# Denominators of two batches inverted once per head, and an order planned with other landing times

## The chip, the cores and the metric

The kernel runs on one core of a Trainium2 chip. Its engines are TensorE (PE, matrix products, with weight loads shown as PEld), VectorE (DVE), ScalarE (ACT), GpSimd (POOL, which here issues the loads) and SyncE (SP, which issues stores and DMA transposes). The metric is the device time of one execution in microseconds, as the median of several runs.

## The reference

Eight batches of eight heads; sequence S = 576, head dimension 64, 32 landmarks (means over 18 neighbouring positions). The attention is approximated through the landmarks, and its output goes through a layer of two products with a silu between them.

```python
m = 32
q_lm = q.reshape(B, H, m, S // m, D).mean(axis=3)
k_lm = k.reshape(B, H, m, S // m, D).mean(axis=3)
A  = sm(q, k_lm)          # softmax of scale * q k_lm^T, over the landmarks
Bm = sm(q_lm, k_lm)
C  = sm(q_lm, k)
Z  = Bm^T / (norms of Bm)
for _ in range(6):
    Z = 2 * Z - Z @ Bm @ Z
attn = A @ Z @ C @ v      # (8, 8, 576, 64)
x = attn.transpose(0, 2, 1, 3).reshape(4608, 512)
h = x @ w_in              # 512 x 2048
out = (h * sigmoid(h)) @ w_out   # 2048 x 512
```

The change concerns the softmax of A: the exponentials exp(scale * q k_lm^T) have to be divided by their sum over the 32 landmarks, for each query position of each head.

## The kernel before

Work goes batch by batch. The eight heads of a batch are two groups (g = 0, 1) of four; four heads times 32 landmarks fill the 128 partitions, so all tiles of the landmark side are "128 x positions". The 576 positions are handled as two halves (c = 0, 1) of HS = 288 columns.

For each batch, `attn(b)` lays down these steps, by the names that they have in the code and with the lines of the profile:

- loads of q, k and v by POOL (`ld...`, `ldv...`, L447 to L460; w_in and w_out L467 to L477);
- the transposed q and k, `qT`: for batches 0 to 2 by PE (L568) and a copy, from batch 3 on by DMA transposes on SP (`xt`, L592), which also wait for the second-last load of the batch's own v;
- landmark sums (`lms` on PE for batches 0 and 1, a tree of additions `red`, L628, on DVE for the others), the landmarks transposed (`ltr`, `lmT`), their product `sb` and its exponential `pb` (L688, L693);
- the iteration for Z: products `ns` on PE and the step `nsd` on DVE (L754), six times in turn;
- for A: products `A`, four exponentials `Ax` on ACT into `et` (L784), four products `S` with a mask of ones, `bones`, so that every one of a head's 32 partitions gets the sum over its landmarks, four logarithms `Ln` on ACT (L794, 288 columns each), two exponentials of minus that, `Rs` (L798, 576 columns each), which gives the reciprocals, and two products on DVE, `etn` (L803, 576 columns);
- for C: products `C`, exponentials `Cx` with their sums (L829), the transposed result `ct` (PE for batches 0 and 1, L844; DMA on SP after that, L856), and the product with v, `cv`;
- the small matrices joined (`wc` L889, `zbd` L894, `zt`), and the product `m` of the result with w_in, copied out by ACT (L404) or DVE (L406).

`layer1(b)` then multiplies `etn` with `m` (`h`, 16 tiles of 512 and two that gather the last 64 columns) and applies the silu on ACT into `gm` and `gx` (L956, L979). `layer2_batch(b)` multiplies by w_out: the first 256 positions of batch 0 plainly, the rest in pairs by seven products in place of eight with sums on DVE (L1044), evacuated by copies and additions (`ost`, L404, L406, L1079) and stored from SP (L1021).

Exponentials and logarithms are in one ACT table and the silu in another, so ACT goes through a group `x{b}` of one batch's exponentials as a whole before it changes the table (`ACT_TABLE_LOAD`, 1.28 us).

The order in which each engine gets its instructions is written by a planner in the kernel, `Plan.run`. It knows a duration for each operation and a lag before its result can be used; whenever an engine is free it picks the ready operation with the lowest priority value. A PE operation is ready only `margin` after its inputs (MARGIN = 0.4 us, nothing for those marked crit). The dict `ORDER` shifts the priority of 52 named operations; `o.done` of a load holds how long after its turn in the queue it lands, `XLAG` the same for DMA transposes. Engines then run their instructions strictly in the planned order, each waiting for its inputs by semaphores. Up to 45 us the planner fills free PE time with a product of zeros, tile `zer`.

`mm` (L394) is the helper of all products and `copy` (L404, L406) of all copies, so that tiles tell more than lines there.

Of the kernel before, what the change touches and what calls it, by code (L numbers as in the profile page):

```python
# [7 lines left out]
FP = mybir.dt.float32  # L8
# [8 lines left out]


ORDER = {
    "f0.0": (200.69, 0), "A.0": (-135.46, 12.93), "Ln11.0": (-57.289, 0), "etn1.0": (-31.554, 0),  # L20
    "ctm00.0": (-1364.2, 0), "wc.0": (-5319.5, 0), "mc11.0": (-629.91, 0), "tr10.1": (-42.668, 0),
    "trc15.1": (-1007.6, 0), "tr19.1": (-457.92, 0), "tr114.1": (-85.703, 0),
    "tr00.1": (-4845.1, 0), "tr09.1": (-1.1208, 0), "tr014.1": (-139.96, 0),
    "lms116.1": (413.98, 0), "lms000.1": (-607.71, 0), "lms006.1": (-83.37, 0),
    "lms010.1": (328.48, 0), "nsd00.1": (-627.38, 0), "ns10.1": (2306.7, 0),
    "nsd10.1": (-1204.8, 0), "A.1": (-266.77, 0), "Ax10.1": (-230.29, 0), "Rs1.1": (-127.11, 0),
    "Cx00.1": (-281, 0), "Cx01.1": (-181.38, 0), "Cx11.1": (-2693.4, 0), "tr014.2": (-314.54, 0),
    "bbd.2": (-120.57, 0), "nsd40.2": (175.02, 0), "h15.1": (234.98, 0), "lrd1.3": (-791.6, 0),
    "A.3": (-480.16, 0), "S00.3": (52.867, 0), "Ln01.3": (24.258, 0), "Ax11.3": (-2.2697, 0),
    "h3.2": (185.78, 0), "hx0.2": (41.862, 0), "h11.2": (452.76, 0), "hx8.2": (-6.3754, 0),  # L30
    "p5@5200.0": (-179, 0), "c12@5220.0": (-251.23, 0), "A.4": (-78.982, 0),
    "etn1.4": (1667.8, 0), "Cx11.4": (29.753, 0), "cv0.4": (-3300.5, 0),
    "p6@5340.0": (-4.9303, 0), "p7@5340.0": (-4146.8, 0), "Ax10.6": (162.02, 0),
    "ss00@5500.0": (-5226.2, 0), "p7@5700.0": (633.04, 0), "p4@5720.0": (524.17, 0),
}


# [29 lines left out]
class Plan:  # L67
# [16 lines left out]
    def run(self):  # L84
# [59 lines left out]
        while n < total:  # L144
# [7 lines left out]
            while moved:  # L152
                moved = False
                for e in ("PE", "ACT", "DVE", "POOL", "SP"):
# [101 lines left out]
                    lag = self.LAG[e] if o.lag is None else o.lag  # L256
                    if o.dma:
                        dmaq[0] = max(dmaq[0], end + 0.1) + o.dma
                        o.done = dmaq[0] + ((2.2 if t < 4.2 else 3.3 if t < 45 else 4.0)
                                              if e == "POOL" else lag)  # L260
                    else:
                        o.done = end + lag
# [39 lines left out]
def act_us(n):  # L302
    return 0.06 + 0.00083 * n
# [6 lines left out]
def mm_us(n, count=1):  # L310
    return count * max(n / 2400 + 0.0025, 0.028)
# [3 lines left out]
def kernel(  # L315
# [24 lines left out]
    SW = 128 + L  # L340
    NPE = 2
    NTR = 3
    SBF = 2
    MERGE = False
    WM = False
    NCT = 2
# [11 lines left out]
    def bank(o, i=0):  # L358
        return banks[o.slot[i]]
# [33 lines left out]
    def mm(out_ap, lhsT, rhs, start=True, stop=True):  # L393
        nc.tensor.matmul(out=out_ap, lhsT=lhsT, rhs=rhs, start=start, stop=stop,  # L394
                         skip_group_check=True)

    def bc(ap, n, axis):
        shape = list(ap.shape)
        shape.insert(axis, n)
        return ap.unsqueeze(axis).to_broadcast(shape)  # L400
# [128 lines left out]
    def folds(e):  # L529
        for r in (0, 64):  # L530
            for c in (0, 64):
                nc.vector.tensor_copy(out=fold[r:r + 64, c:c + 64], in_=idb[r:r + 64, r:r + 64])
    cfold = A("fold", [("DVE", 0.6)], folds, [cid], 90.0)


# [6 lines left out]
    def attn(b):  # L542
# [41 lines left out]
        else:  # L584
# [3 lines left out]
            for t in (1, 0):  # L588
                for g in range(NG):
                    qt_ops[t, g] = [A(  # L590
                        f"xt{t}{g}.{b}", [("SP", 1.38)],
                        lambda e, t=t, g=g: nc.sync.dma_start_transpose(  # L592
                            out=qT[:, t, g], in_=qk[:, t, g].rearrange("p j d -> p (j d)")),
                        [qk_ops[b, t, g]] + use + gate, p0 + 5, lag=XLAG)]
                    qt_ops[t, g][0].after = gate
                    me["qk_read"] += qt_ops[t, g]
                    me["xts"] += qt_ops[t, g]
# [170 lines left out]
        def am(e):  # L768
            for g in range(NG):
                for h in range(4):  # L770
# [5 lines left out]
                    lmT_all + ([] if cr else [(pb_op, -0.2)]) + qt_ops[0, 0] + qt_ops[0, 1] + ready, p0 + 20,  # L776
                    psum=4, tiled="q")
        me["A"].opens = grp
        for g in range(NG):
            et, ln = et_r[g], ln_r[g]  # L780
            lns = []
            for c in range(2):
                x = A(f"Ax{g}{c}.{b}", [("ACT", act_us(HS))],
                      lambda e, g=g, et=et, c=c: nc.scalar.activation(  # L784
                          out=et[:, c], in_=bank(me["A"], 2 * g + c)[:, 0:HS], func=AF.Exp,
                          scale=sc / J),
                      [me["A"], prev.get(f"etn{g}")], p0 + 21 + g, table="exp",
                      group=grp).reads(me["A"], 2 * g + c)
                me["S", g, c] = A(f"S{g}{c}.{b}", [("PE", mm_us(HS))],
                                  lambda e, g=g, c=c, et=et: mm(  # L790
                    bank(me["S", g, c])[:, 0:HS], bones, et[:, c]), [x, c0],
# [32 lines left out]
        for g in range(NG):  # L824
# [29 lines left out]
            else:  # L854
                ct_ops[g] = [A(f"ct{g}.{b}", [("SP", 1.38)], lambda e, ce=ce, ct=ct:
                               nc.sync.dma_start_transpose(  # L856
                                   out=ct, in_=ce.rearrange("p i x -> p (i x)")),
                               xs + [prev.get("cv")] + v_ops.get(b + 1, [])[-2:-1], p0 + 20, lag=XLAG)]
                ct_ops[g][0].after = v_ops.get(b + 1, [])[-2:-1]
                me["cts"] += ct_ops[g]  # L860

# [285 lines left out]
    for b in range(B + 1):  # L1147
        if b < B:
            attn(b)
        if b:  # L1150
            layer1(b - 1)
            layer2_batch(b - 1)

    order = P.run()
    if PLAN_DUMP is not None:
        PLAN_DUMP(order)
# [49 lines left out]
```

## Time and profile before

| what | value |
|---|---|
| median of 5 runs | 247.59 us (247.41 to 248.87) |
| the profiled execution | 248.87 us |
| its span, first to last instruction | 247.0 us |
| what lies around the span | 1.87 us |
| mean granted clock of TensorE | 0.997 |
| busy: PE, DVE, ACT, POOL | 239.6, 171.9, 183.4, 37.3 us |
| ACT_TABLE_LOAD | 12 (6 to the exponentials' table, 6 to the silu's), 1.28 us each |
| read from HBM, written | 36.70 MB, 9.44 MB |

A row of the profile's table of groups gives the line, the engine, the operation, the tiles written and read, the shapes, the count, and then the busy time and the mean duration of one. Instructions overlap: the next one of an engine can start before the one ahead is done, so what an instruction takes of its engine's time is the distance from its start to the next start. The ends of products on PE are modelled, and a filler counts as busy.

### The profile page before, as it was taken

How to read it: one execution, taken by the hardware profiler on the slowest of the kernel's cores; microseconds unless marked ns; L12 is line 12 of the kernel's file. 1: busy time of each engine (PE TensorE's matmuls, PEld its weight loads, DVE VectorE, ACT ScalarE, POOL GpSimd, SP SyncE). 2: the span in 40 equal slices, each digit the busy share in tenths (PEclk: the TensorE clock that was granted, in tenths of full speed). 3: DMA queues.
4: the chain of work that ended last, by engine and by line, in shares of the span. 5: the costliest groups of instructions: out<-in, count | busy, mean ns of one | idle time of the engine just before them, and what ended most of it. 6: DMA issues, size and time to landing. Idle time of an engine off the chain costs nothing.

```text
span 247.0 us, 7075 instructions
## 1 busy us (share of the span) xinstructions
PE 239.6 (97%) x2771; PEld 171.2 (69%) x2771; DVE 171.9 (70%) x441; ACT 183.4 (74%) x438; POOL 37.3 (15%) x63
## 2 busy tenths in 40 slices
PE   8999999999979999999999999999999999999993
PEld 6877565565867655577886655697886566688883
DVE  2368956495869957949999879189798667066632
ACT  2587997499866999997668998966988978922200
POOL 8426833300022002200220050000000000000000
PEclk9999999999999999999999999999999999999998
DMA  6999999999889969989899799896453003022352
GB/s 102 196 203 196 189 207 206 207 241 180 170 120 201 227 139 163 199 144 161 167 235 225 159 172 231 149 167 109 105 123 96 0 3 85 3 73 59 86 140 73
DMA packets 55873, 36.50 MB, mean 148 GB/s; under 512 B 36640, under 2 KB 47392, under 8 KB 55840
## 3 DMA queue, kind: packets, MB, share of 16 engines
q0 software_dynamic: 15264, 18.35, 44.7%
q1 hardware_dynamic: 39808, 16.92, 32.9%
q10 hardware_dynamic: 768, 0.79, 1.3%
q8 instruction: 21, 0.34, 0.5%
q14 instruction: 12, 0.10, 0.1%
HBM read 36.70 MB, written 9.44 MB: 187 GB/s over the span
## 4 chain that ended last, share of the span: by engine, by line
PE 83%; DMA 7%; ACT 3%; DVE 3%; issue 1%; POOL 1%; SPq 1%; POOLq 0%; DVEq 0%
PE ps L394 81%; DMA qk<-in_k_dram 4%; DMA qT<-qk 2%; PE ps L568 2%; POOL qk L447 1%; ACT m L404 1%; SPq L592 1%; PE ps L844 1%; DVE st L754 1%; ACT ce L829 1%; DVE red L628 1%; ACT L956 1%; ACT ln L794 0%; DVE etn L803 0%; DVE ss L1044 0%
## 5 line engine op out<-in xcount | busy, mean ns | idle before, releaser
L394 PE MATMUL ps<-etn,m 128*128 128x512 bf16 (+1 forms) x512 | 68.9, 286 | 0.4 <-ACT gm L956 0.4
L956 ACT ACTIVATE gm<-ps 128x512 f16<-128x512 f32 x128 | 66.0, 648 | 2.0 <-PE ps L394 1.8
L394 PEld LDWEIGHTS <-gm 128*128 128x128 f16 x512 | 48.7, 98 | 11.3 <-issue 2.4
L394 PE MATMUL ps<-w_out_sb,gm 128*128 128x256 f16 (+1 forms) x392 | 53.6, 281 | 0.0
L394 PEld LDWEIGHTS <-m 128*128 128x128 bf16 x512 | 32.0, 98 | 24.1 <-issue 1.8
L404 ACT COPY ost<-ps 128x256 f32<-128x256 f32 (+1 forms) x48 | 18.5, 385 | 37.3 <-PE ps L394 28.9
L394 PEld LDWEIGHTS <-ss 128*128 128x128 f16 x408 | 39.1, 98 | 6.6 <-issue 0.9
L1079 DVE TENSOR_TENSOR ost<-ost,ps 128x256 f32<-128x256 f32 x51 | 21.2, 417 | 20.3 <-PE ps L394 14.2
L394 PE MATMUL ps<-wt,ss 128*128 128x256 f16 x272 | 34.0, 273 | 0.0
L754 DVE SCALAR_TENSOR_TENSOR st<-st,ps 128x320 bf16<-128x320 bf16 (+3 forms) x54 | 21.5, 405 | 9.1 <-PE ps L394 6.8
L406 DVE CAST m<-ps 128x512 bf16<-128x512 f32 x31 | 20.1, 685 | 0.7 <-PE ps L394 0.5
L406 DVE COPY ost<-ps 128x256 f32<-128x256 f32 x22 | 9.3, 423 | 15.5 <-PE ps L394 14.8
L404 ACT CAST m<-ps 128x512 bf16<-128x512 f32 x33 | 17.9, 603 | 1.7 <-PE ps L394 1.7
L394 PE MATMUL ps<-w_out_sb,ss 128*128 128x256 f16 x136 | 17.6, 273 | 0.0
L453 POOL DMA_DIRECT2D qk<-in_k_dram x7 | 5.0, 715 | 81.6 <-DMA ct<-ce 41.1
L460 POOL DMA_DIRECT2D v<-in_v_dram x24 | 14.0, 590 | 15.0 <-PE ps L394 7.5
L394 PE MATMUL ps<-zer 128*128 128x256 bf16 x79 | 14.7, 310 | 1.1 <-DVE zer L487 1.1
L394 PE MATMUL ps<-wt,gm 128*128 128x256 f16 x120 | 15.5, 272 | 0.0
L394 PEld LDWEIGHTS <-st 128*128 128x128 bf16 x96 | 8.4, 97 | 8.9 <-issue 2.9
L394 PE MATMUL ps<-st 128*128 128x160 bf16 (+1 forms) x96 | 14.4, 225 | 0.2 <-DVE wsb L889 0.2
L829 ACT ACTIVATE ce<-ps 128x288 bf16<-128x288 f32 x32 | 12.9, 414 | 0.0
L404 ACT COPY qT<-ps 128x640 bf16<-128x640 bf16 (+1 forms) x12 | 7.9, 690 | 6.1 <-PE ps L568 6.0
(91 smaller groups left out, 335.2 us busy)
## 6 DMA issues: line engine op xcount, KB each, us to landing
out_dram<-ost SPq DMA_DIRECT2D x128, 64.0 KB, 2.0
v<-in_v_dram POOLq DMA_DIRECT2D x24, 192.0 KB, 11.3
qk<-in_k_dram POOLq DMA_DIRECT2D x7, 576.0 KB, 6.6
qk<-in_q_dram POOLq DMA_DIRECT2D x7, 576.0 KB, 10.4
w_out_sb<-in_moe_w_out_dram POOLq DMA_DIRECT2D x4, 512.0 KB, 10.5
w_in_sb<-in_moe_w_in_dram POOLq DMA_DIRECT2D x4, 256.0 KB, 8.4
w_in_sb<-in_moe_w_in_dram POOLq DMA_DIRECT2D x8, 128.0 KB, 7.1
qk<-in_k_dram POOLq DMA_DIRECT2D x2, 288.0 KB, 4.3
```

The costliest lines, as they stand in the source:

```text
L394: nc.tensor.matmul(out=out_ap, lhsT=lhsT, rhs=rhs, start=start, stop=stop, skip_group_check=True)
L404: nc.scalar.copy(out=out, in_=in_)
L406: nc.vector.tensor_copy(out=out, in_=in_)
L447: lambda e, t=t, g=g, src=src: nc.gpsimd.dma_start(out=qk_r[b % 2][:, t, g].rearrange("p j d -> p (j d)"), in_=src[b][4 * g:4 * g + 4].rea ...
L453: lambda e, t=t, src=src: nc.gpsimd.dma_start(out=qk_r[b % 2][:, t].rearrange("p g j d -> p g (j d)"), in_=src[b].rearrange("(g h) (l j) d ...
L460: lambda e, a=a: nc.gpsimd.dma_start(out=v_r[b % 2][a * L:(a + 1) * L, :, :], in_=v[b].rearrange("h (l a x) d -> a l h (x d)", l=L, a=VA)[ ...
L568: nc.tensor.transpose(out=ps[:, n * 128:(n + 1) * 128], in_=qk[:, t, g, 2 * jp:2 * jp + 2, :].rearrange("p j d -> p (j d)"), identity=idb)
L592: lambda e, t=t, g=g: nc.sync.dma_start_transpose(out=qT[:, t, g], in_=qk[:, t, g].rearrange("p j d -> p (j d)")),
L754: nc.vector.scalar_tensor_tensor(out=s2[:, g0:g1, lo:SW], in0=s[:, g0:g1, lo:SW], scalar=2.0, in1=ps[:, 0:NG * SW].rearrange("p (g x) -> p ...
L829: nc.scalar.activation(out=ce[:, :, 0:VP].rearrange("p (i c) (a l) -> p c a i l", c=2, a=VA)[:, c], in_=bank(me["C"], 2 * g + c)[:, 0:HS]. ...
L956: lambda e, dc=dc, cell=cell: nc.scalar.activation(out=gm[:, dc, :], in_=bank(cell["o"]), func=AF.Silu),
L1079: nc.vector.tensor_tensor(out=out_, in0=x, in1=y, op=OP.add)
```

## The change

Three things change.

The denominators of A, for batches 0 and 1 only (`NRC`). The four `S` products now write one tile between them: each of the four (g, c) pairs takes 32 partitions of it, eight for each head, by using every fourth column of `bones`. One Ln and one exponential of 288 columns then give the reciprocals of all of them at once (with a factor of 8 in it, since each stands on eight partitions). `sel`, a matrix of zeros and ones made once from the identity, spreads them by PE to the 32 partitions of each head; so that little precision is lost in bf16, the reciprocal is split into a bf16 part (`Rh`) and the rest, also in bf16 (`Rl`), and PE adds the two (HILO). The four `etn` products read the spread reciprocals straight from PSUM.

```diff
+    NRC = (0, 1)
+    HILO = True
...
+    def sels(e):
+        nc.vector.reduce_sum(out=pbs_r[0][:, 0:8].rearrange("p a g -> p (a g)"),
+                             in_=idb.rearrange("p (a x) -> p a x", x=8), axis=AX.X)
+        nc.vector.tensor_copy(out=sel, in_=bc(
+            pbs_r[0][:, 0:8].rearrange("p (a c) g -> p a (c g)", c=2), L, 3))
+    csel = A("sel", [("DVE", 0.85)], sels, [cid], -98.0)
...
+        if b in NRC:
+            rcp = ln_r[b % 2][:, 0]
+            def sm(e):
+                for g in range(NG):
+                    for c in range(2):
+                        r = L * (2 * g + c)
+                        mm(bank(me["S"])[r:r + L, 0:HS], bones[:, 0:128:4], et_r[g][:, c])
+            me["S"] = A(f"S00.{b}", [("PE", mm_us(HS))], sm, list(ax.values()) + [c0], p0 + 22,
+                        psum=1, tiled="s")
+            x = A(f"Ln00.{b}", [("ACT", act_us(HS))], lambda e: nc.scalar.activation(
+                out=rcp, in_=bank(me["S"])[:, 0:HS], func=AF.Ln, scale=8.0), [me["S"]]
+                + [prev.get("etn0"), prev.get("etn1")], p0 + 25, table="exp", group=grp).reads(me["S"])
+            x = A(f"Rs0.{b}", [("ACT", act_us(HS))], lambda e: nc.scalar.activation(
+                out=rcp, in_=rcp, func=AF.Exp, scale=-1.0), [x], p0 + 25.1, table="exp",
+                group=grp)
...
+                x = A(f"Rh.{b}", either(HS), lambda e: copy(e, rhl[:, 0], rcp), [x], p0 + 26)
+                x = A(f"Rl.{b}", [("DVE", dve_us(HS))], lambda e: nc.vector.tensor_tensor(
+                    out=rhl[:, 1], in0=rcp, in1=rhl[:, 0], op=OP.subtract), [x], p0 + 26)
...
+                        for u in range(2):
+                            mm(bank(me["R", g, c])[:, 0:HS], w, rhl[:, u], start=(u == 0),
+                               stop=(u == 1))
...
+                    me[f"etn{g}{c}"] = A(f"etn{g}{c}.{b}", [("DVE", dve_us(HS))],
+                                         lambda e, g=g, c=c: nc.vector.tensor_tensor(
+                        out=etn[:, g, HS * c:HS * c + HS], in0=et_r[g][:, c],
+                        in1=bank(me["R", g, c])[:, 0:HS], op=OP.mult),
+                        [me["R", g, c], l1_done.get(b - 2)], p0 + 30).reads(me["R", g, c])
...
-        for g in range(NG):
+        for g in range(NG if b not in NRC else 0):
             et, ln = et_r[g], ln_r[g]
```

The planner's times. Loads planned before 7.4 us are taken to land 2.0 us after their turn (before: 2.2 for those before 4.2 us); the transposes of q for batch 3 get 1.2 us more, other `xt` 0.1, the `ct` of batch 2 0.8. PE's steps for batches 0 and 1, without layer 1, `m`, `zt` and `cv` of batch 1, get a margin of at most 0.1 us.

```diff
-                        o.done = dmaq[0] + ((2.2 if t < 4.2 else 3.3 if t < 45 else 4.0)
+                        o.done = dmaq[0] + ((2.0 if t < 7.4 else 3.3 if t < 45 else 4.0)
...
+                        lag=XLAG + (1.2 if b == 3 and not t else 0.1))]
...
+                               lag=XLAG + (0.8 if b == 2 else 0.0))]
...
+    EARLY = 0.1
...
+    for o in P.ops:
+        if o.engs[0][0] == "PE" and (o.name[-2:] == ".0" or o.name[-2:] == ".1" and not
+                                     o.name.startswith(("h", "m", "zt", "cv"))):
+            o.margin = min(o.margin, EARLY)
```

The dict ORDER. All of its entries are replaced (52 before, 71 after), so that the order of work can differ anywhere in the kernel. The first line of each:

```diff
-    "f0.0": (200.69, 0), "A.0": (-135.46, 12.93), "Ln11.0": (-57.289, 0), "etn1.0": (-31.554, 0),
...
+    "lms016.0": (296.86, 0), "ns00.0": (-1682.2, 0), "ns20.0": (183.81, 0),
...
```

## The prediction

> **What bounds the kernel now.** I read the page's busy shares first, then busy time by stage, the chain that ended last, and the order of work on ScalarE (ACT), VectorE (DVE) and the DMA queues. The page makes TensorE (PE) the bound:
>
> ```profile
> PE 239.6 (97%) x2771; PEld 171.2 (69%) x2771; DVE 171.9 (70%) x441; ACT 183.4 (74%) x438; POOL 37.3 (15%) x63
> PE 83%; DMA 7%; ACT 3%; DVE 3%; issue 1%; POOL 1%; SPq 1%; POOLq 0%; DVEq 0%
> ```
>
> An average over stages that differ, though. The table by stage (columns: length, then busy time and count of PE, weight loads, DVE, ACT, POOL; clock; DMA):
>
> ```profile
> 0.00:15.00 15.00, 13.47 (x204) 10.53 (x205) 5.50 (x27) 6.65 (x18) 7.89 (x17) 1.00 0.89 159
> 15.00:35.00 20.00, 19.96 (x315) 13.67 (x312) 16.28 (x50) 18.24 (x48) 11.92 (x18) 1.00 1.23 197
> 35.00:52.00 17.00, 17.00 (x190) 9.80 (x189) 9.82 (x19) 11.60 (x25) 4.92 (x8) 1.00 1.22 210
> 52.00:62.00 10.00, 10.00 (x89) 6.01 (x87) 7.08 (x17) 10.00 (x21) 0.00 (x0) 1.00 1.05 201
> 62.00:71.00 9.00, 9.00 (x111) 7.30 (x109) 6.79 (x23) 7.25 (x24) 0.00 (x0) 1.00 1.01 148
> 71.00:89.00 18.00, 16.05 (x204) 11.46 (x202) 16.94 (x46) 14.20 (x39) 3.15 (x5) 1.00 0.92 184
> 89.00:243.00 154.00, 153.81 (x1676) 112.44 (x1675) 109.05 (x261) 115.50 (x271) 9.43 (x15) 1.00 0.65 127
> ```
>
> [...]
>
> ```profile
> 15.00:35.00 20.00, 6.46 (x36) 3.12 (x36) 0.00 (x0) 1.00 1.23 197
> ```
>
> 36 fillers between 15 and 35 us; one streams 256 columns in about 0.11 us (six in a row end 0.82 us after the first began, with 0.27 us for one alone), so some 3.9 us of PE there is idle time in disguise. The engine that is really full is ACT, 18.24 of 20 us. Its order of work:
>
> ```profile
> 16.97 1.33 ACT L794 ACTIVATE ln<-ps 128x288 f32<-128x288 f32 x4
> 18.15 1.29 ACT L798 ACTIVATE ln<-ln 128x576 f32<-128x576 f32 x2
> 30.68 1.28 ACT L956 ACT_TABLE_LOAD   x1
> 31.98 0.60 ACT L956 ACTIVATE gm<-ps 128x512 f16<-128x512 f32 x1
> ```
>
> Layer 1 of batch 0 cannot put out its first silu before batch 1's exponentials end (30.67) and the table is loaded. So stage 1 (13 to 42 us) is ACT's; stage 2 (35 to 71) is PE's, without a filler and almost without a gap; stage 3 begins with a transfer:
>
> ```profile
> 65.87 5.48 DMA qT<-qk
> 71.47 0.69 DVE red L628
> 89.19 154.09 PE ps L394 x1676
> ```
>
> Batch 3's q and k are transposed by DMA from 61.60, when the second-last load of its v has landed (61.44). Then DVE is full (16.94 of 18) until layer 1 of batch 2 starts its silus at 88.54, and from 89 us PE runs to the end. Whatever brings 88.54 forward by x brings the end forward by about x.
>
> **Part 1, ACT in batches 0 and 1.** Per batch four Ln of 288 and two exponentials of 576 go; one Ln and one exponential of 288 come. By start-to-start times, four Ln take 18.15 - 16.97 = 1.18 us (0.295 each) and the two wide ones 19.30 - 18.15 = 1.15. New: 2 x 0.295 = 0.59. Saved 1.74 us a batch, 3.48 in two. The bf16 copy of the reciprocal (Rh) may run on ACT (0.30, like an Ln of this width) or DVE (0.37 by part 2's spacing); on ACT it leaves 1.44 a batch. ACT waits only 0.29 + 0.78 + 0.65 + 0.28 = 2.0 us between 12.96 and 41.8, so the saving is on that stage's path. All of batch 1's arrives at 30.68 (1.44 to 1.74); batch 0's arrives only if batch 1's group then opens before 22.98, which needs PE's sums of q and k to come sooner. Bounds 0.6 (the wait for PE grows instead) to 3.5; I take **2.0 us**.
>
> **Part 2, DVE.** Two products of 576 (start to start 0.665, so 1.33) become four of 288 that read PSUM. Two 128-column products out of PSUM start 0.20 us apart (20.627, 20.828), so 288 columns take 0.20 + 160 x 1.04 ns = 0.37, four 1.47: +0.14. The low part (Rl) adds 0.30 + 0.07 = 0.37, Rh as much if it comes here. So +0.5 to +0.9 a batch. From 24 to 32 us DVE is nearly full (7.57 of 8 us by its rows), so batch 1's share counts: I charge 0.3 of it, the rest goes where ACT takes over casts of m. The selector matrix (a reduction and a copy to 512 columns: 0.22 for a reduction of 64 elements and 0.68 for a cast of 512, so about 0.9) is built beside the folds at 4.06, in DVE's first 7 us, which are idle but for constants: 0, and at most 0.9 if that gap were closed.
>
> [...]
>
> **Part 3, PE.** S: eight products of 288 (0.123 apart: 16.301, 16.424, 16.546) become eight on 32 columns each, four side by side: -0.98 and, with a mode change at either end, +0.3 to +0.65. The spread adds 16 x 0.123 = 1.97. Net about +1.5 us, under the 3.9 us of fillers: cost 0; without that cover, 1.5. The eight spread products wait on DVE's Rl, and what is queued behind them on PE waits too: batch 1's iteration steps and the first m products. A late Rl costs about 0.4 us (one DVE step) a batch; I charge 0.1. The longer path to etn (two more DVE steps and a product, about +1.5 us) costs nothing: etn of batch 0 is ready at 20.7 and wanted at 29.71, batch 1's is ready at 31.9 and wanted at 52.
>
> **Part 4, the order.** EARLY lets the plan place PE's work for batches 0 and 1 0.3 us sooner after its inputs (0 to 0.5 gained, I take 0.1: most of it waits for loads). The transfers keep their sizes and sequence, and the queue runs at about 200 GB/s throughout, so w_out lands at 33.3 to 40.95, v of batch 1 at 43.92, v of batch 3 at 61.44 as before. The new landing lags and the new ORDER re-sort everything after; PE's gaps after 89 us are small in any one place. From the page I cannot tell the sign: 0, with +-1.0.
>
> **The sum.** Stage 1: 2.0 - 0.3 - 0.1 + 0.1 = 1.7 us earlier. Stage 2 passes it: PE is full there, layer 2 of batch 0 has w_out landed for three of its four pieces by 38.44, and the floor set by v (43.92, plus 5 us of steps to a silu) is 4.4 us below the present 53.34. At stage 3 the transposes do not move, but DVE has 2.2 us idle before 71 in a stage of 9 and none after: batch 2's steps and layer 2's sums, come 1.7 earlier, fit into that hole and leave the full stretch. I pass all of it. The profiled execution took 248.87 (span 247.0 and 1.87 around it), 1.28 above the median of five, 247.59. So 248.87 - 1.7 = 247.17 for it, and 247.59 - 1.7 = **245.9** for the median. About 0.5% (1.2 us) is what a measurement of this kernel can tell from no change.
>
> **Rivals.**
> *The second gate eats it.* The transposes at 61.60 and the chain behind them (reduce, landmarks, exponentials, table, 17 us) set 88.54 alone; what comes earlier waits there. For: PE already runs dry in stage 3 (16.05 of 18). Against: DVE's 94% there. Time 247.59 + (0 to 0.3), less a little: 247.4.
> *Slower: stores in front of the loads.* One mechanism: layer 2 of batch 0 finishes its second pair sooner, so its stores are put ahead of the transposes. Eight stores at 46.80 to 50.93 already stand between loads: three v and k of batch 3 took 56.87 - 49.72 = 7.15 us where undisturbed 3 x 1.0 and 2.9 make 5.9, so eight stores cost 1.25 us of landing. Eight more move 61.44, hence 88.54, by 1.3, and the sequencer blocks up to 4.55 us behind them if their data is late. It decides once those stores stand before 61.6 in SP's queue; today the next ones leave at 71.57. With a mispacked PE queue behind 89 us (+0.4): 249.2.
> *It does not do what it says:* PE's spread products wait on DVE so long that ACT, relieved, waits for PE. Then the first silu stays at 31.98 and the time at 247.6; I count it with the first rival.
>
> **Chances and range.** Carried through 0.52 (own range 244.0 to 246.3: up to 3.5 from stage 1); eaten or not delivered 0.22 (246.4 to 248.8); slower 0.26 (248.9 to 250.5, by the store mechanism or by a worse order). Leaving out the upper part of the last and the lowest tail: 244.0 to 249.3.
>
> **What would show it.** Right: four ACT rows a batch gone, first silu near 30.0, fewer than 25 fillers between 15 and 35, batch 1's first silu near 51.6, transposes still near 61.6, layer 1 of batch 2 near 86.8. Wrong: first silu before 30 but batch 2's still at 88.5 (first rival); transposes after 62.5 with more than eight stores before them (second); PE idle before spread products with ACT waiting on PE (third). More than 2 us lost or gained after 89 us would make the order, not the denominators, the cause.

## The result, and the profile after

The median went from 248.42 us (43 runs of before beside it) to 249.32 us (22 runs): ratio 1.0045, 95% interval 1.0029 to 1.0061. I had predicted 245.9, from a median of 247.59 in the five runs of before that I knew; as a ratio that is 0.993. The profiled execution after took 249.44 us, span 247.7, against 248.87 and 247.0.

The page after, busy shares and the chain that ended last:

```profile
PE 239.8 (97%) x2773; PEld 170.7 (69%) x2773; DVE 173.1 (70%) x448; ACT 179.8 (73%) x431; POOL 37.3 (15%) x63
...
PE 87%; DMA 5%; DVE 4%; POOL 1%; ACT 1%; issue 1%; POOLq 0%
```

The stage table (length; busy time and count of PE, weight loads, DVE, ACT, POOL; clock; DMA share; GB/s):

```profile
0.00:15.00 15.00, 12.92 (x214) 10.47 (x215) 5.99 (x28) 6.42 (x13) 8.61 (x18) 1.00 0.89 159
15.00:35.00 20.00, 19.64 (x304) 13.12 (x301) 16.75 (x55) 17.54 (x47) 11.18 (x17) 1.00 1.24 201
...
62.00:71.00 9.00, 9.00 (x110) 7.31 (x109) 8.27 (x26) 7.83 (x26) 0.00 (x0) 1.00 1.05 163
71.00:89.00 18.00, 17.30 (x221) 12.29 (x220) 17.17 (x45) 13.73 (x39) 3.15 (x5) 1.00 0.98 203
```

ACT is relieved in sum (179.8 against 183.4) but hardly in 15 to 35 us, 17.54 against 18.24. The hole in PE after 71 us, 16.05 of 18 before, is nearly closed. The fillers of 15 to 35 us, tile zer in the same table (PE, weight loads, DVE), went from 36 to 26:

```profile
15.00:35.00 20.00, 4.48 (x26) 2.21 (x26) 0.00 (x0) 1.00 1.24 201
```

Milestones of the two profiled executions (us from the span's start), read from the order of work on ACT and PE:

| | before | after |
|---|---|---|
| first silu of batch 0 | 31.98 | 31.81 |
| from there to batch 1's first silu | 21.36 | 21.91 |
| to batch 2's | 35.20 | 34.20 |
| to batch 3's | 11.99 | 12.85 |
| to the end of PE's last product | 142.74 | 142.18 |
| to the end of the span | 3.75 | 4.78 |
| around the span | 1.85 | 1.71 |

The differences sum to +0.57: -0.17 + 0.55 - 1.00 + 0.86 - 0.56 + 1.03 - 0.14. "Silu" in the rows is the first silu that ACT does for that batch. There are three questions in the table: why the first silu did not come 1.7 us sooner, what moves the two middle rows, and what the last stores lost.

### The profile page after: what moved, and what is told of

It reads as the page before. It is cut to its first block, busy times and chain, and to the rows that moved or that the text cites. A ratio compares the mean times of both kernels' runs of the same rounds, so it can differ in the third digit from the quotient of the medians.

```text
span 247.7 us, 7097 instructions
## 1 busy us (share of the span) xinstructions
PE 239.8 (97%) x2773; PEld 170.7 (69%) x2773; DVE 173.1 (70%) x448; ACT 179.8 (73%) x431; POOL 37.3 (15%) x63
## 3 DMA queue, kind: packets, MB, share of 16 engines
HBM read 36.70 MB, written 9.44 MB: 186 GB/s over the span
## 4 chain that ended last, share of the span: by engine, by line
PE 87%; DMA 5%; DVE 4%; POOL 1%; ACT 1%; issue 1%; POOLq 0%
PE ps L403 85%; DMA qk<-in_q_dram 5%; PE ps L587 1%; DVE m L415 1%; POOL qk L456 1%; DVE etn L870 1%; DVE st L774 1%; PE ps L911 0%; ACT ln L861 0%; ACT ct L413 0%; POOL qk L462 0%; DVE ss L1112 0%; ACT ln L865 0%; DVE ost L415 0%; DVE wsb L957 0%
## 5 line engine op out<-in xcount | busy, mean ns | idle before, releaser
L403 PE MATMUL ps<-etn,m 128*128 128x64 bf16 (+1 forms) x512 | 69.2, 286 | 0.5 <-DVE m L415 0.5
L403 PE MATMUL ps<-w_out_sb,gm 128*128 128x256 f16 (+1 forms) x392 | 52.9, 281 | 0.0
L413 ACT COPY ost<-ps 128x256 f32<-128x256 f32 (+1 forms) x51 | 19.6, 385 | 37.5 <-PE ps L403 33.9
L403 PEld LDWEIGHTS <-ss 128*128 128x128 f16 x408 | 38.6, 98 | 9.1 <-issue 2.7
L413 ACT CAST m<-ps 128x512 bf16<-128x512 f32 x35 | 18.8, 596 | 3.5 <-PE ps L403 3.5
L415 DVE CAST m<-ps 128x512 bf16<-128x512 f32 x29 | 19.0, 685 | 1.1 <-PE ps L403 1.0
L415 DVE COPY ost<-ps 128x256 f32<-128x256 f32 x19 | 8.0, 422 | 14.3 <-PE ps L403 14.1
L403 PE MATMUL ps<-zer 128*128 128x256 bf16 x65 | 11.4, 306 | 1.1 <-DVE zer L496 1.1
```

The lines of the kernel that those rows point to most:

```text
L413: nc.scalar.copy(out=out, in_=in_)
L415: nc.vector.tensor_copy(out=out, in_=in_)
```

## The experiments

Ratios are to the kernel before, in runs on the same chip, with 95% intervals. "The stage" is the time from batch 1's first silu to batch 3's.

**The last stores.** In the kernel after, the last two stores (issued at 243.99 by SP and at 244.34 by ACT; at the end of both kernels every second store goes out from ACT, not only from SP as said above) have their last landings at 246.57 and 246.74, where 15 of the 16 DMA engines are done by 245.82. DMA queues from 245 us to the end (packets, MB, share of 16 engines), after:

```profile
q10 hardware_dynamic: 48, 0.03, 4.5%
q1 hardware_dynamic: 36, 0.02, 2.7%
q14 instruction: 1, 0.01, 0.7%
```

One block of 8 KB of instructions is fetched there, at 245.4. The pages count one more packet on that queue, before and after:

```profile
q14 instruction: 12, 0.10, 0.1%
q14 instruction: 13, 0.11, 0.1%
```

Five of the 13 come when ACT has started 66, 186, 322, 443 and 577 of the instructions that its trace records, 128 apart on average. After has 580 of these, before 568, and the program 584 and 572: only after reaches the fifth block. That they are ACT's code was a guess, so I lengthened its stream.

e1, the kernel after with 16 copies more:

```diff
+            if o.name == "const":
+                padt = constp.tile([128, 64], BF, tag="padt", name="padt")
+                for i in range(16):
+                    nc.scalar.copy(out=padt[:, i:i + 1], in_=zer[:, i:i + 1])
```

> The changed kernel with 16 copies of one column added on ACT in its idle time before 6 us; nothing else differs. In the profile of the changed kernel a fetch of 8 KB on the queue of instructions begins at 245.4 us, while the last two stores are written, and one of 16 DMA engines lands its part of the last store at 246.74 where the other fifteen land by 245.82; the profile before has no fetch after 233.1 us. Theory 'a late fetch' (ACT's stream grew from 572 to 584 instructions, so that a block more of it is fetched at the very end): 16 instructions earlier in the stream, the fetch comes before 243 us, the last store lands with all engines within 0.3 us, and the time falls by 0.7 to 1.0 us, to a ratio of 0.998 to 1.001 to the kernel before. Rival 'the order is slower' (the loss of 0.45% lies in the work itself): the ratio stays at 1.003 to 1.006.

Measured: 1.0001 (0.9978 to 1.0024), 248.52 us. The block came at 238.7, the last store landed at 245.76, PE's end stayed (243.00). The milestones before it agree with after's within 0.06 us. So the measured loss of the change sits in the last stores, and against before as it runs all the rest of it together cannot be told from nothing (within some 0.6 us either way).

e2, the kernel before with 12 such copies:

> The kernel before with 12 one-column copies added on ACT in its idle time before 7 us, which brings its ACT stream from 572 to the 584 instructions of the changed kernel; order and work are otherwise the same. 'A late fetch': a thirteenth 8 KB fetch on that queue appears after 240 us, one DMA engine lands its part of a last store about 0.9 us after the others, the span grows by 0.7 to 1.0 us and the ratio is 1.003 to 1.004. 'The order is slower': no such fetch matters, ratio 0.999 to 1.001.

Measured: 0.9982 (0.9959 to 1.0005), 248.06 us. The block did appear, at 245.1, and the last store landed at 246.44; the ratio lies below both ranges. Two things meet in it. From PE's end to the end of the span it took 4.76 us where before took 3.75, the same 1.0 us that e1 takes away from after. But PE ended 0.61 sooner (242.66), for which the part on the middle has a reason.

The other profiles say the same. From PE's end to the span's end it is 3.72 to 3.76 us in the nine whose last ACT block came before 240 us (before, e1, e3, f1, f2, g1, j1, j3, k2), and 4.33 to 4.78 in the six where it came after 244 (after, e2, e4, f3, j2, k1), in both orders. (In h1, 7 us longer, it is 4.06.)

**Stage 1: where the relief of ACT went.** e3 keeps the old order and leaves out three of the four logarithms and their part of the exponentials in batches 0 and 1 (the remaining reciprocal divides all four parts), which is ACT's new amount of logarithms and exponentials without the new steps:

```diff
+    KEEP = {0: (0, 0), 1: (1, 0)}
...
+                             lambda e, g=g, c=c, ln=ln: (nc.scalar.activation(
+                                 out=ln[:, c], in_=bank(me["S", g, c])[:, 0:HS], func=AF.Ln)
+                                 if b > 1 or (g, c) == KEEP[b] else None),
...
+                if g == KEEP[b][0]:
+                    h = ln[:, KEEP[b][1]]
+                    return nc.scalar.activation(out=h, in_=h, func=AF.Exp, scale=-1.0)
```

> The kernel before in its own order, with ACT's work for the denominators of batches 0 and 1 cut to what the changed kernel has: one Ln and one exponential of 288 columns a batch in place of four and of two with 576; the same reciprocals are used for all four parts, so the other three denominators are left out. PE and DVE do what they did. Theory of the prediction (ACT sets stage 1): batch 0's first silu comes 1.4 to 3.0 us before 31.98, and since PE has fillers there and is full after it, the end comes 1.0 us or more earlier, ratio 0.993 to 0.997. Rival 'ACT's freed time turns into waiting for PE and for landings': first silu within 0.8 us of 31.98, ACT's waits between 15 and 32 us grow by 2 us or more, ratio 0.998 to 1.001.

Measured: 1.0005 (0.9978 to 1.0031). ACT's order of work in it (start, duration, what; in brackets the idle time before):

```profile
24.59 1.32 ACT L785 ACTIVATE et<-ps 128x288 bf16<-128x288 f32 x4 [0.65 <-PE ps L394]
...
27.11 0.41 ACT L841 ACTIVATE ce<-ps 128x288 bf16<-128x288 f32 x1 [0.90 <-DVE bbd L711]
...
30.65 1.28 ACT L968 ACT_TABLE_LOAD   x1
31.94 0.60 ACT L968 ACTIVATE gm<-ps 128x512 f16<-128x512 f32 x1
```

In before, the same group opens like this:

```profile
22.98 0.22 ACT L688 ACTIVATE pb<-ps 128x64 f32<-128x64 f32 x1 [0.78 <-PE ps L394]
23.85 1.32 ACT L784 ACTIVATE et<-ps 128x288 bf16<-128x288 f32 x4 [0.65 <-PE ps L394]
```

From batch 1's first exponential to the first silu e3 takes 7.35 us (31.94 - 24.59) where before took 8.13 (31.98 - 23.85): 0.78 of batch 1's 1.74 (no Rh here). The rest of the relief became a wait of 0.90 for `bbd`, DVE's block-diagonal matrix that the iteration starts from. In this execution PE stood 0.70 us among batch 0's value products (at 22.53; the waits put it down to issue, that is to nothing the profile shows), and batch 1's first exponential came 0.74 later; that hid the 0.78 in the milestone, so this kernel alone could not decide.

f1 and f2 bring the loads forward: two of the three loads of batch 0's v are left out (its values for them are zeros), which puts later loads forward: batch 3's transposes start 1.8 (f1) and 2.5 us (f2) sooner than in before. f2 has e3's relief as well.

```diff
-  lambda e, a=a: nc.gpsimd.dma_start(
+  lambda e, a=a: None if not b and a else nc.gpsimd.dma_start(
```

> The kernel before in its own order with two of the three loads of batch 0's v left out (0.38 MB, about 2.0 us of the load queue by the landings 18.18, 19.22, 20.18 of the three; zeros stand there instead, set by DVE before 6 us). All later loads should land 2 us sooner (last part of w_in near 28.8 in place of 30.80, v of batch 1 near 41.9). Theory L, 'the landings of the loads pace the first 45 us, ACT does not': the end moves with them, 1.0 to 2.0 us sooner, ratio 0.992 to 0.996. Theory A (the prediction's: ACT, full from 15 to 31, paces it): first silu within 0.5 us of 31.98, ratio 0.998 to 1.001.

Measured: 0.9933 (0.9905 to 0.9961), 246.98 us, which is theory L's ratio but not for its reason. The first silu stays at 31.84 and batch 1's at 53.20. The gain comes later: batch 3's transposes start at 59.84 instead of 61.60 and the stage takes 45.26 instead of 47.19.

> The order of the kernel before, with two loads of batch 0's v left out and ACT's work for the denominators cut to one Ln and one exponential of 288 columns a batch (three of four denominators left out). The loads alone gave 0.9933 [0.9905, 0.9961], ACT's relief alone 1.0005 [0.9978, 1.0031]. Theory L (landings pace the first 45 us): no better than with the loads alone, 0.991 to 0.996. If ACT and loads each hold the other up: both together give 2.5 us or more, ratio 0.990 or less.

Measured: 0.9914 (0.9882 to 0.9946), 246.15 us; first silu 30.57, batch 1's 52.62, the stage 45.26. Against f1 the relief brings the first silu 1.27 us forward and batch 1's only 0.58. (The two ratios differ by less than their intervals.) PE runs without a gap in between; 0.35 of the lost 0.69 is six transposes of ce, and most of the rest the end of eight m products (0.15) and two steps of the iteration (0.14), work that stood before the silu and now stands behind it. What comes forward at the silu is not what comes forward on PE.

In the kernel after, ACT is relieved too; here is its order of work:

```profile
24.57 1.01 ACT L804 ACTIVATE et<-ps 128x288 bf16<-128x288 f32 x3 [1.35 <-PE ps L403]
25.78 0.37 ACT L413 CAST zt<-ps 128x256 bf16<-128x256 f32 x1 [0.20 <-PE ps L403]
...
30.04 0.45 ACT L413 CAST ln<-ln 128x288 bf16<-128x288 f32 x1
30.51 1.28 ACT L1024 ACT_TABLE_LOAD   x1
31.81 0.60 ACT L1024 ACTIVATE gm<-ps 128x512 f16<-128x512 f32 x1
```

From the first exponential to the silu 7.24 us: 0.89 saved, the rest spent on copies that the plan gave to ACT (zt was DVE's before; Rh is the row at 30.04). And the exponentials begin 0.72 later than before (24.57 against 23.85), after a wait of 1.35 for PE, though the group opens with pb at 22.96 as before (22.98). 0.89 - 0.72 = 0.17, which is the whole change of the milestone.

What is PE late with? Its order of work there (columns as for ACT, with the shape of the stationary operand behind the tiles):

```profile
23.03 0.53 PE L403 MATMUL ps<-v,ct 96*64 96x128 bf16 x12
...
23.61 0.53 PE L403 MATMUL ps<-v,ct 96*64 96x128 bf16 x12
...
24.19 0.44 PE L403 MATMUL ps<-qT,lmT 64*32 64x288 bf16 x16
```

The sums A.1, which the exponentials read, stand behind batch 0's 24 value products. f3, with f1's edit in the kernel after, asks whether loads gate the new order, k1 whether this place does.

> The changed kernel in its own order with the same two loads of v left out. Theory L: it gains as much as the kernel before does (0.0067, 1.7 us), ratio to the kernel before 0.996 to 1.000, with the late fetch still in its end. Theory A, by which the changed order has freed ACT and waits for loads alone: it gains more than the kernel before does, 2 us, ratio 0.994 to 0.996.

Measured: 1.0028 (1.0006 to 1.0049), 249.07 us. First silu 31.63, the transposes start at 59.50, and the stage stays at 47.05. The new order takes next to nothing from earlier loads.

k1 moves those products behind A.1; k2 adds e1's copies:

```diff
+    mv = [x for x in order if x[0].name in ("cv0.0", "cv1.0")]
+    order = [x for x in order if x not in mv]
+    at = [x[0].name for x in order].index("A.1")
+    order[at + 1:at + 1] = mv
```

> The kernel after with batch 1's sums of q and k (A.1, 16 products) put on TensorE ahead of batch 0's value products (cv0.0 and cv1.0, 24 products), nothing else changed. Theory Q (the relief turned into a wait for TensorE because of this place in the queue): batch 1's first exponential at 23.4 to 23.7 us instead of 24.57, first silu at 30.8 to 31.4 instead of 31.81; as TensorE is full from there and the order behind it is fixed, the whole moves with it: ratio to before 1.000 to 1.003. Rival R (another gate, m's casts or the spread products, holds the silu): exponentials earlier, first silu 31.7 to 31.9, ratio 1.003 to 1.006.

Measured: 1.009 (1.0066 to 1.0114), 250.61 us.

```profile
24.55 1.02 ACT L804 ACTIVATE et<-ps 128x288 bf16<-128x288 f32 x3 [1.17 <-PE ps L403]
26.83 0.37 ACT L413 CAST zt<-ps 128x256 bf16<-128x256 f32 x1 [1.26 <-PE ps L403]
...
32.86 0.60 ACT L1024 ACTIVATE gm<-ps 128x512 f16<-128x512 f32 x1
```

Both theories on record fall. The exponentials are as late as before the move, so the place behind the value products was not their gate. PE's order of work shows what is:

```profile
23.46 0.19 PE L403 MATMUL ps<-st 128*128 128x32 bf16 x1 [0.18 <-DVE st L774]
24.05 0.19 PE L403 MATMUL ps<-st 128*128 128x32 bf16 x1 [0.41 <-DVE st L774]
24.17 0.44 PE L403 MATMUL ps<-qT,lmT 64*32 64x288 bf16 x16
```

The last two steps of batch 0's iteration stand in front of A.1 and wait 0.59 us in all for DVE; in the kernel after the value products only filled these waits. The old order had A.1 (23.35) ahead of these two steps (25.04 and 25.27). Putting A.1 back in front of them was not tried. zt comes 1.05 later, and the first silu exactly 1.05 later. The new order is tight at batch 0's chain to zt as well. Every later milestone moves by the same 1.05.

> The same, with 16 one-column copies added on ScalarE before 6 us, so that its last 8 KB instruction fetch comes some 8 us before the last stores instead of among them. If both theories hold (Q's 0.4 to 1.0 us and the 0.9 us of the last store): ratio to before 0.996 to 0.999. If only the stores': 0.999 to 1.002.

Measured: 1.0038 (1.0018 to 1.0058), 249.31 us, 1.3 us below k1, so the copies help here too. In the profiles the time from PE's end to the span's end is 3.73 against 4.33, which explains half of it; the other half is open. First silu 33.05.

e4 takes the low part out of the new denominators (no Rl, one spread product instead of two, so the reciprocal is only bf16):

> The changed kernel in its own order without the low part of the reciprocal: Rl on DVE and the second product of each pair on PE are left out (4 products a batch in place of 8, one DVE step less). Theory 'the longer chain costs': the last etn product of batch 0, which batch 1's A products are made to wait for, moves up by 0.5 to 1.0 us from 23.14, batch 1's first exponential from 24.57 to 23.6 to 24.1, and the first silu by 0.4 to 1.0 from 31.81; ratio to the kernel before 1.001 to 1.003 (the late fetch stays, since ACT's stream keeps its 584 instructions). Theory of the prediction (the added steps lie under other work): first silu within 0.2 of 31.81, ratio 1.004 to 1.005.

Measured: 1.0046 (1.0023 to 1.0069); the first silu at 32.64 (in this execution PE waited 1.1 us for the load of k), then 21.91, 34.20 and 12.85 as in after. The added steps' amount is not what the new kernel pays for. Where four of batch 1's eight spread products are gone, fillers took their place (behind the first silu 0.96 us of them against 0.58).

h1 makes only the denominators new and leaves ORDER, the landing lags and the margins of before:

> The denominator part alone: the new Ln, exponential, split, spread and products for batches 0 and 1, with the landing times, margins and ORDER of the kernel before, so that the plan is made again by shifts that were not meant for it. If the denominators' part by itself is worth anything apart from the order: ratio 0.993 to 1.000. If the order decides and its shifts fit only the step list they were made for: 1.005 to 1.03.

Measured: 1.0283 (1.0251 to 1.0315), 255.56 us. Its losses lie along the whole span (batch 2's first silu 91.48, and PE ends 147.8 after batch 3's where it takes 142.7 in before). As I read it, the shifts in ORDER fit the list of steps that they were chosen for; the new denominators cannot be priced alone this way.

**The middle: what a fourth transpose costs.** Before's two middle rows vary with the experiment, after's never. In before, the fourth transpose of batch 3 is in flight from 65.87 to 71.35. The DMA queues in that window, and the median time from issue to landing:

```profile
q1 hardware_dynamic: 2991, 0.75, 108.0%
q8 instruction: 1, 0.02, 2.0%
qT<-qk SPq DMA_TRANSPOSE x1, 5.5
```

A block of 16 KB on the queue q8 is fetched at 68.62 and takes 1.76 us; 17 of the transpose's packets, begun behind it at 69.06 to 69.36, took 1.8 to 2.1 us each, where between 61 and 68.5 us none of the 4539 of that size (256 bytes) took over 0.14. That queue's 21 packets come about 250 recorded PE instructions (products and weight loads) apart, 252 on average, so I took them for PE's code; by ACT's 8 KB for some 128 instructions, 16 KB are some 256, the figure in j1's expectation below. Whoever waits on the transfer that the block meets pays for it: here 5.48 us from issue to landing, where the transpose before took 3.36.

A sign of it had come with g1, an attempt to move ACT's fetches out of the middle with 28 copies on ACT in the old order, 14 at the start and 14 behind batch 0's last silu:

> The kernel before with 28 one-column copies on ACT, 14 before 7 us and 14 in its idle time after batch 0's last silu (41.8 to 46.2), which brings its ACT stream to 600 instructions, as many as the changed kernel has with 16. Against 12 such copies (ratio 0.998, with a fetch at 245.1 that held up one engine's part of the last store by 0.9 us), this puts the thirteenth fetch near 239 us. If a late fetch costs about 0.9 us in every execution and early copies on ACT somehow gain as much, this gives 0.993 to 0.996. If the copies do nothing and the late fetch costs little in this kernel, 0.998 to 1.001.

Measured: 0.9942 (0.9915 to 0.9970), 247.16 us: faster than both kernels. Its stage took 45.77. The transposes began at 61.09 and the fourth had landed (68.35) when PE's block came at 69.32. The start alone is no effect of the copies: where the loads are left alone it varies from 60.91 (k1) to 62.83 (e3), and in e2, with copies, it is 61.65.

But the four kernels with copies (e1, e2, g1, k2) have something else in common. Each of batch 3's four transposes takes them 2.90 to 3.05 us from issue to landing; in all the others one that meets no block takes 3.25 to 3.68. In e2 the fourth, issued at 65.87 as in before, had landed at 68.81, when a block had only just begun (68.5). So e2 and g1 are sooner in the middle for this reason at least. The edit brings a new tile, `padt`, along with the instructions; which of the two shortens the transposes was not tried.

j1 and j3 move PE's blocks alone, in the old order: j1 by 180 instructions earlier (ten fillers of the start cut into ten products of one column each), j3 by 18 later (18 fillers joined into nine).

```diff
+            if o is P.filler:
+                k += 1
+                if 8 < k <= 18:
+                    for i in range(10):
+                        mm(banks[7][:, 0:1], zer[:, 0:128], zer[:, 0:1])
+                    continue
```

> The kernel before with ten of its early fillers (8 to 18 of the start's zeros) each cut into ten products of one column, which adds 180 TensorE instructions before 7 us and changes nothing else. TensorE's 16 KB instruction fetches, about one per 256 instructions, then come some 180 instructions earlier in its work: in the profile of before those at 68.6 and 94.2 us would fall near 62 and 86, the next ones near 74 and 96. Theory F (a fetch that falls on batch 3's or batch 4's transposes delays the fourth of them, and TensorE waits): the fourth transpose of batch 3 lands within 16 us of batch 1's first silu, batch 1's first silu to batch 3's takes 45.3 to 45.8 instead of 47.2, ratio to before 0.991 to 0.996. Rival S (the spread of before comes from the landings of its loads and the copies added on ScalarE gained by something else): ratio 0.999 to 1.002, the stage still 46 to 47.2.

Measured: 0.9987 (0.9961 to 1.0013), 248.35 us. The blocks came at 61.6, 71.3, 83.9 and 94.1. Between them the fourth transpose of batch 3 needs (same view, the transpose's window)

```profile
qT<-qk SPq DMA_TRANSPOSE x1, 3.4
```

and the chain of waits no longer goes through it:

```profile
52.88 25.57 PE ps L394 x281
...
78.48 0.42 DVE ost L1079
...
87.93 45.93 PE ps L394 x537
```

PE works 25.57 us without a wait where before's chain had the transfer at 65.87, and the stage takes 45.26 (99.27 - 54.01), as theory F said. The time missed its range; one reason is that the cut fillers held PE up at the start (PE's first products on k start at 5.90 instead of 5.37, and the first silu came at 32.64, 0.66 later). The mechanism is confirmed, the gain is not.

> The kernel before with its first 18 fillers joined into nine of 512 columns, which takes 18 TensorE instructions away: the fetch at 68.6 us comes 0.7 us later, at 69.3, after the fourth transpose of batch 3, and that at 94.2 us falls on batch 4's third transpose. Theory F: batch 1's first silu to batch 2's takes 33.3 instead of 35.2, batch 2's to batch 3's 12.0 to 13.0 instead of 12.0; ratio 0.994 to 0.998, between before and the kernel with 180 more. Rival S: no change, 0.999 to 1.002.

Measured: 0.9980 (0.9954 to 1.0006), 247.73 us; batch 1's first silu to batch 2's 33.27, batch 2's to batch 3's 13.27. The block that missed batch 3's transposes fell on batch 4's second one, at 91.6 (issued 89.53, landed 94.28), and now the chain goes there:

```profile
51.60 25.57 PE ps L394 x281
...
89.53 4.75 DMA qT<-qk
...
94.38 0.69 DVE red L628
```

All eight profiles of the old order fit one rule, for the two stages alike (all times from the first silu of the stage; "4th" is the landing of the fourth transpose):

| old order | batch 3's 4th | stage | batch 4's 4th | stage |
|---|---|---|---|---|
| f2 | 14.01 | 33.27 | 6.24 | 11.99 |
| f1 | 14.45 | 33.27 | 7.59 | 11.99 |
| g1 | 15.12 | 33.27 | 9.44 | 12.50 |
| j1 | 15.35 | 33.27 | 8.83 | 11.99 |
| e2 | 15.83 | 33.29 | 10.90 | 13.66 |
| j3 | 15.85 | 33.27 | 10.43 | 13.27 |
| e3 | 16.13 | 33.31 | 10.43 | 13.53 |
| before | 18.01 | 35.20 | 9.11 | 11.99 |

Up to 16.1 and 9.1 us a landing cost at most 0.04 us; past that each microsecond costs about one. In the new order, after, e1, e4, f3 and j2 have landings of 13.6 to 17.0 and 9.7 to 10.9, and each takes 34.20 to 34.21 and 12.84 to 12.86.

> The kernel after with the same cut of ten early fillers. Theory F with the new order planned for late landings: the stage from batch 1's first silu to batch 3's stays 47.05 whenever the transposes land, so the ratio to before stays 1.003 to 1.006. Rival: the new order gains from a free transpose too, stage 45.3 to 46.2, ratio 0.997 to 1.001.

j2, j1's edit in the kernel after. Measured: 1.0076 (1.0048 to 1.0105), 250.63 us. The ratio is above the range since the first silu is 1.09 later, with the same cut fillers; batch 3's fourth transpose landed early (14.65), and the stage is 47.05 as ever:

```profile
54.34 20.76 PE ps L403 x208
...
75.12 0.49 DVE st L774
```

So the new plan waits for nothing at these landings and can use no earlier one. The new lags (1.2 us more for batch 3's later transposes, 0.8 for ct of batch 2) would make such a plan; whether they or the new shifts did, no run separates. Against the old order undisturbed (33.27 + 11.99 = 45.26) its stage is 1.79 us longer, against before's profiled execution 0.14 shorter. The fairest pair on record is g1 and e1, both with copies and neither with a block among the last stores: 0.9942 for the old order, 1.0001 for the new, some 1.5 us, of which 1.28 is the stage (45.77 and 47.05). They ran on different chips, each beside before. The new order's times are also steadier: the middle half of the spans lies within 0.3 to 0.4 us in after (247.3 to 247.6) and e1 (246.5 to 246.9), within 1.0 to 1.2 in before (246.0 to 247.2). That before's own spread comes from these meetings is what the table suggests; no run varied them alone over many executions.

## Why the prediction was wrong

Of the 3.4 us between 245.9 and 249.32, 0.8 is the base (247.59 in five runs, 248.42 in 43). The rest is nearly the 1.7 us that did not come and the 0.9 us lost at the end.

**Part 1, ACT's relief (2.0 us earlier): wrong, 0.17.** This is the step that failed: that ACT's saving lies on stage 1's path because ACT hardly waits there. The rows were counted rightly. In batch 1 only 0.89 of 1.44 to 1.74 arrived, as ACT took over zt's copy and Rh, and in batch 0 the sign was wrong: its exponentials came 1.2 us earlier (13.43 against 14.66), but batch 1's group opened where it did (22.96) and its exponentials came 0.72 later, since PE's A.1 stood behind batch 0's iteration steps, which wait for DVE (k1). My lower bound, "the wait for PE grows instead", was the answer, and more than I allowed for. I read 2.0 us of waits in a full ACT as proof that ACT sets the end; e3 and f2 show other gates (waits of 0.65 for PE's sums and 0.90 for DVE's bbd) within a microsecond behind it, and e3, the relief alone, measured 1.0005.

**Part 2, DVE: right in the rows.** Two new products start 0.364 us apart (20.319, 20.683; the last two of the three below), for which I had 0.37 from the rows. The 1.04 ns a column in that estimate is in the rows of before as well: the product whose spacing of 0.20 I used takes 280 ns on 128 columns and 414 on 256, 1.05 ns a column (L736, means of 2 and of 7). The new products, after:

```profile
19.96 1.18 DVE L845 TENSOR_TENSOR etn<-et,ps 128x288 bf16<-128x288 bf16 x3
```

**Part 3, PE: partly wrong.** The fillers fell from 36 to 26, just above the "fewer than 25" that I had given. The mode change is in the rows of before: a filler takes 0.11 us to the next start, and 0.20 where the next product is tiled 64*32 (23.15 to 23.35). The four S products of a batch after start within 0.01 us of each other and take 0.25 to the next start (15.21 to 15.46, 26.93 to 27.18), with 0.09 more in front of the first four: 0.59 for two batches, inside my 0.3 to 0.65. But "batch 1's etn is wanted at 52" did not cover its spread products: they run between 31.74 and 33.36 and take 0.97 us of PE by their starts (0.24 + 0.73), and layer 1's next product (etn, m) starts at 33.44 instead of 32.80. "The longer path to etn costs nothing" also missed that batch 0's last etn slipped to 23.14 on DVE, where it stands right in front of the iteration steps that A.1 and zt wait for. PE's rows, the last one of before, and DVE's:

```profile
31.74 0.41 PE L403 MATMUL ps<-ln,red 128*128 128x288 bf16 x2
31.98 0.60 PE L403 MATMUL ps<-zer 128*128 128x256 bf16 x4
32.46 0.90 PE L403 MATMUL ps<-ln,red 128*128 128x288 bf16 x6
33.19 0.30 PE L403 MATMUL ps<-st 128*128 128x160 bf16 x2
...
33.44 1.51 PE L403 MATMUL ps<-etn,m 128*128 128x512 bf16 x6
```

```profile
32.80 1.03 PE L394 MATMUL ps<-etn,m 128*128 128x512 bf16 x4
```

```profile
23.14 0.45 DVE L845 TENSOR_TENSOR etn<-et,ps 128x288 bf16<-128x288 bf16 x1
23.51 0.41 DVE L774 SCALAR_TENSOR_TENSOR st<-st,ps 128x160 bf16<-128x160 bf16 x2
```

**"Stage 2 passes it": wrong.** f2 passed 0.58 of 1.27. The silu's time is no measure of PE's.

**Stage 3 and Part 4, the order (0 +-1.0): the sum near, by luck.** Transposes stayed near 61.6 as said (61.67), batch 2's first silu came at 87.92, not 86.8. The rule that whatever brings it forward brings the end forward failed as well: it came 0.62 sooner and PE ended 0.32 sooner, as batch 3's row grew by 0.86. The chain of before showed the transfer of 5.48 us, and I took that as its normal length; the three before it take 3.4 (61.60 to 64.96), as the fourth does in j1 with no block in its window, and the difference was the code fetch. In before's profile it cost 1.93 us in that stage (35.20 - 33.27), more than the whole forecast gain, and it was there without the change.

**Left out altogether: the last stores.** +1.03 us in the profile, 0.0044 in the ratio between after and e1. Of the rivals, "slower" (248.9 to 250.5) has the number, but its one mechanism, stores in front of the loads, did not happen (61.67). What the first stage shows is nearest to the third: the silu hardly moves and ACT waits 1.35 us for PE. But there PE was to wait in front of its spread products, and it waited in front of iteration steps; leaving out half of the spread products (e4) changed nothing.

## What to carry to other kernels

Before pricing a relief, look for the second gate: the idle row in front of the next chain and who ends it, since a stage that is 91% busy may have three limits within 1 us, as ACT's here (18.24 of 20 us, with waits of 0.65 for PE and 0.90 for DVE behind it in e3). Compare a transfer in the chain with its neighbours of the same shape; the one that was 2 us longer here (5.48 against 3.4) had met something, and the order should either miss that or be planned for the late landing, at the price of the early one. An experiment that adds instructions or a tile can move code fetches and change transfers (e1: ACT's last block from 245.4 to 238.7, batch 3's transposes, where they meet no block, 2.90 to 3.05 us with the copies and 3.25 to 3.68 without), so look at what else its trace has that is new. Shifts chosen for one list of steps are part of that list, so a change of steps under the old shifts (h1, 1.0283) prices neither.

## What the runs showed of the hardware

A dozen instructions more on ACT, at its start, lengthened the end of a kernel by 1.0 us (e2, 4.76 us from PE's end, where before took 3.75): ACT's next 8 KB of code came in the middle of the last stores (at 245.1). In after the same block came at 245.4, one of 16 DMA engines landed its part 0.9 us after the others (246.74 against 245.82), and the end took 4.78 us; with the block at 238.7 (e1) it took at most 3.76. PE's blocks of 16 KB took mostly 0.9 to 1.0 us and up to 1.76 (21 each in before and after), and a transpose that met one landed 1.3 to 2.1 us late in three cases (after: 66.01 + 3.44 would be 69.45, and it was 70.76; j3: 89.53 + 3.27, as the one before it took, would be 92.8, and it was 94.28; before: 65.87 + 3.36 would be 69.2, and it was 71.35). Not every transpose in flight is held up: e1's fourth, from 65.68 to 68.60, took its usual 2.92 with a block from 68.0. Which transfer was met changed with the number of PE instructions in front of it, so fillers, which do nothing, decided it: before's block met batch 3's fourth transpose, with 180 instructions more none came while that one was in flight (j1), and with 18 fewer a block met batch 4's second (j3).
